# Bias attention with a cosine FFN: two V bursts per unit, one group of q/k transposes per slot

## The chip, the cores and the metric

The kernel runs on one core of a Trainium2 chip. The metric is device time in microseconds (us), the median of the runs shown; a profile comes from one further execution. TensorE is called PE in the profile, VectorE DVE, ScalarE ACT, GpSimd POOL, and SyncE, which issues the DMAs, SP. PEld is PE's loading of weights.

## The reference

All inputs are float32. Attention has 4 batches, 8 heads, 576 positions, head width 64; a small network over log-distances gives a bias for each head. Then an FFN with a cosine gate follows on 2304 tokens of width 512.

```python
scores = scale * np.matmul(q, k.transpose(0, 1, 3, 2))
x = (psi_rel / psi_i)[..., None]
bias = np.maximum(x @ w1 + b1, 0.0) @ w2
scores = scores + bias.transpose(2, 0, 1)[None, :, :, :]
attn = np.exp(scores - np.max(scores, axis=-1, keepdims=True))
attn = attn / (np.sum(attn, axis=-1, keepdims=True) + 1e-09)
out = np.matmul(attn, v)
h = x_attn @ w_in                # x_attn: out, heads side by side
result = (h * np.cos(h)) @ w_out
```

## The kernel before

Three stages follow one another. The first (to about 79 us) computes the bias table and stores it in DRAM. The second (to about 387 us) is attention, and the change lies there. The third is the FFN.

Attention works on **units**: a unit is a pair of heads (`hp`) of one batch (`b`), 16 in all, numbered 0 to 15 with the batch running fastest. A unit has five **slots**, one for each tile of queries, `tiles = [0, 1, 4, 2, 3]`: four tiles of 128 queries for each of the two heads, and tile 4, which holds the 64 left-over queries of both heads. The order of instructions is written out by hand in `slot(i)`, which software-pipelines three jobs. In slot i:

- PE computes the scores of the slot's own job (`qk`, L378, into `s`; two heads, so two tiles of two banks each, from a pool of two). DVE adds the bias and takes the minimum (L389, `neg` and `m`); the sign is turned.
- For the job of the slot before, ACT takes the exponentials (`softmax_exp`, L408), DVE adds to the sums and inverts them (`recip`, L420 and L423), and POOL multiplies (`norm`, L430).
- For the job before that, PE transposes P: eight transposes (L437, four for each head) and the left-over one (L442). The first head's four are copied to `PT` by ACT, the second head's by DVE (`keep_main`, L450 and L453), and the left-over one to `PX` by DVE.

Beside these stand four more kinds of work. The V matmuls (`pv`, L494) multiply PT and PX with V. The first half of a unit's queries has 256 columns and the second 320, and each half needs five chunks of keys: 0 to 3 from PT, 4 from PX. The two heads share the array, 64 columns each. When chunk 4 is done ACT copies the sum to `xT`. The q and k of the next unit are transposed (`turn`): `k0`, `k1`, `q0`, `q1` are four transposes for one head (`tmain`, L195, copied by ACT at L202), `kl` and `ql` are the left-over ones (`tleft`, L206, copied by ACT at L208 to L212). `swap` issues two DMAs that copy k with its halves exchanged (`kS`, L216 and L217). POOL splits q and k of coming units (`split`, L172 and L176), following `POOL_PLAN`, SP loads them (`LOAD_PLAN`), and `W_PLAN` spreads the widening of FFN weights over pairs of units: the raw load in slot 1 of even units, the absolute value on ACT in slot 0 of odd ones, DVE's steps in slots 1 and 2 of odd ones (L99, L100, L102, L104). In units 3, 7 and 11 (`b == B - 1`) every slot also loads a bias tile of the next pair of heads.

All transposes, of P as of q and k, write to one pool of three PSUM banks (`ps_t`, the name `pt` in the rows); the V sums have one bank (`ps_v`). A tile can be written when the copy out of the one three allocations earlier is done. Each engine runs its instructions in the order of the code.

The plans say what stands where. `T_EARLY` is issued between the scores and the P transposes, `T_PLAN` after the slot's copies; likewise `PV_EARLY` and `PV_PLAN`. An entry `(-1, 0, (2, 3, 4))` is: of the unit before, half 0, chunks 2 to 4. In code the V matmuls of half 0 begin at the end of slot 4 (two chunks) and end in slot 0 of the next unit (three); those of half 1 begin at the end of slot 2 and end in slot 3.

Of the kernel before, what the change touches and what calls it, by code (L numbers as in the profile page):

```python
# [28 lines left out]
def kernel(  # L29
# [42 lines left out]
    NU = len(units)  # L72
# [37 lines left out]
    with tc.manual_schedule():  # L110
# [103 lines left out]
        def kswap(u):  # L214
            t = tp.tile([128, 1216], F32R, tag="kS", name="kS")
            nc.sync.dma_start(out=f(t[0:64]), in_=f(kN[u][64:128]))  # L216
            nc.sync.dma_start(out=f(t[64:128]), in_=f(kN[u][0:64]))  # L217
            kS[u] = t

        def turn(u, ops):  # L220
            if u >= NU:
                return
            for op in ops:
                if op == "swap":
                    kswap(u)
                elif op[1] == "l":
                    tleft(u, op[0])
                else:
                    tmain(u, op[0], int(op[1]))
# [135 lines left out]
        def qk(u, j, h):  # L365
            t = tiles[j]
            s = ps_s.tile([128, 2, 512], F32, tag="s", name="s")
            if t < 4:
                o = 128 * t + 704 * h
                stats = [(qTs[u % 2][:, o : o + 128], h)]  # L370
            else:
                stats = [(qTs[u % 2][:, 512:640], 0), (qTs[u % 2][:, 576:704], 1)]
            for hf in range(2):
                n = 0
                for a, hh in stats:
                    c0 = HALF * hf + (640 if t == 4 else 576) * hh
                    for kt in (kN, kS):
                        nc.tensor.matmul(  # L378
                            s[:, hf, 0:HALF],
                            a,  # L380
                            kt[u][:, c0 : c0 + HALF],
                            start=(n == 0),
                            stop=(n == 2 * len(stats) - 1),
                        )
                        n += 1
            hp = units[u][0]
            neg = tt.tile([128, 2, HALF], F32, tag="neg", name="neg")
            m = sv.tile([128, 2], F32, tag=f"m{h}", name="m")
            nc.vector.tensor_tensor_reduce(  # L389
                neg,  # L390
                s[:, :, 0:HALF],
                bias[hp, t, h].rearrange("p (a x) -> p a x", a=2),
                1.0,
                3.0e38,
                ALU.add,
                ALU.min,
                m[:, 0:1],
            )
            cur[u, j, h] = (neg, m)
# [85 lines left out]
        def pv(u, hf, chunks):  # L485
            hp, b = units[u]
            n = vN[u % 2]
            if 0 in chunks:
                X_[u, hf] = ps_v.tile([128, 512], F32, tag="v", name="pv")
            ps = X_[u, hf]  # L490
            for c in chunks:
                for h in range(2):
                    a, m = (n[:, 4 * h + c], PT[u, hf][:, h, c, :]) if c < 4 else (n[:, 8 + h], PX[u, hf])
                    nc.tensor.matmul(  # L494
                        ps[64 * h : 64 * h + 64, 0 : WQ[hf]],
                        a,
                        m,
                        start=(c == 0),
                        stop=(c == 4),
                        tile_position=(0, 64 * h),  # L500
                        skip_group_check=True,
                    )
            if 4 in chunks:
                c0 = b * S + 256 * hf
                act_copy(xT[:, hp, c0 : c0 + WQ[hf]], X_.pop((u, hf))[:, 0 : WQ[hf]])
# [6 lines left out]
            [(2, "k", 1)],  # L512
            [(2, "k", 2)],
        ]
        T_EARLY = [["k0"], ["kl", "swap"], ["q0"], ["ql"], ["q1"]]
        T_PLAN = [["k1"], [], [], [], []]
        PV_EARLY = [[(-1, 0, (2, 3, 4))], [], [], [(-1, 1, (2, 3, 4))], []]
        PV_PLAN = [[], [], [(-1, 1, (0, 1))], [], [(0, 0, (0, 1))]]
        LOAD_PLAN = [[(2, "k")], [], [], [(2, "q")], [(1, "v")]]
        W_PLAN = [("load", 1), ("abs", 5), (0, 6), (1, 6), (2, 7), (3, 9), (4, 9)]  # L520
        get = lambda i: jobs[i] if 0 <= i < len(jobs) else None
# [2 lines left out]
        def slot(i):  # L524
            u, j = divmod(i, 5)
            now, last, prev = get(i), get(i - 1), get(i - 2)
            heads = lambda x: range(2 if tiles[x[1]] < 4 else 1)
            if now:
                qk(u, j, 0)
            if last:  # L530
                for h in heads(last):
                    softmax_exp(*last, h)
            if now and tiles[j] < 4:
                qk(u, j, 1)
            for du, hf, chunks in PV_EARLY[j]:
                if 0 <= u + du < NU:
                    pv(u + du, hf, chunks)
            turn(u + 1, T_EARLY[j])
            if i == 1:
                load_bias(0, tiles[-1])  # L540
            if prev:
                if j in (2, 4):
                    alloc_half(prev[0], j // 2 - 1)
                pt = [ptrans(*prev, h) for h in heads(prev)]
                pl = ptrans_left(*prev)
            if last:
                recip(*last, 0)
                recip(*last, 1)
            if prev:
                if len(pt) == 2:  # L550
                    keep_main(*prev, 0, pt[0])
                    keep_main(*prev, 1, pt[1])
                else:
                    keep_both(prev[0], pt[0])
            if last:
                for h in heads(last):
                    norm(*last, h)
            if prev:
                keep_left(*prev, pl)
            for du, hf, chunks in PV_PLAN[j]:  # L560
                if 0 <= u + du < NU:
                    pv(u + du, hf, chunks)
            turn(u + 1, T_PLAN[j])
            if now:
                for du, x, step in POOL_PLAN[j]:
                    if u + du < NU:
                        split(u + du, x, step)
                for du, x in LOAD_PLAN[j]:
                    if u + du < NU:
                        load(u + du, x)  # L570
                hp, b = units[u]
                if b == B - 1 and hp + 1 < HP:
                    load_bias(hp + 1, tiles[j])
                if u == NU - 1 and j < KD:
                    split_x(0, 0, j)
                for step, at in W_PLAN:
                    w, r = divmod(i - 0 - at, 10)
                    if r == 0 and 0 <= w < len(wparts):
                        if step == "load":
                            load_w(*wparts[w])  # L580
                        elif step == "abs":
                            abs_w(*wparts[w])
                        else:
                            widen_w(*wparts[w], step)
# [226 lines left out]
```

## Time and profile before

| | |
|---|---|
| runs | 800.36, 799.08, 800.66 us; median 800.36 |
| profiled execution | 803.56 us, of which the span from first to last instruction is 801.7 |
| busy, share of the span | PE 764.9 us (95%), PEld 619.2 (77%), DVE 598.4 (75%), ACT 459.1 (57%), POOL 415.4 (52%) |
| granted clock of PE | 0.995 over the span |
| attention, 79 to 387 us | PE busy 286.96 us of 308 |
| V matmuls, L494 | 512 with PT, 128 with PX |
| chain that ended last | PE 81%, ACT 7%, DMA 4%, DVE 4% |

A busy PE is a sum of intervals in which some matmul was under way; since matmuls overlap, what a group costs is read from its start to the start of the next group. The chain of waits is followed back from the last instruction, at each step to what released it. In a timeline row the first number is the start in us, the second the time from the group's first start to its last end; `x8` is the number of instructions in the row, and the bracket tells how long the engine was idle before and what ended that. An fp32 V matmul is two instructions in the trace, so a chunk of both heads is `x4`.

### The profile page before, as it was taken

Reading aid. Unit: us, or ns where it says so; the run is one execution under the profiler, and the core shown is the slowest. Engines: PE = TensorE matmul, PEld = TensorE weight load, DVE = VectorE, ACT = ScalarE, POOL = GpSimd, SP = SyncE. Lnnn points to the kernel's source line nnn. Section 1 sums busy time; section 2 is a strip of 40 time slices with the busy share of each in tenths; the row PEclk is TensorE's granted clock in tenths of the full one; section 3 lists DMA queues with packets and bytes.
Section 4 is the critical chain, followed back from the end, with each engine's and each line's share of the span. In section 5 each row is a group of like instructions: output and inputs, shape, how many; then the busy total and the mean of one; then the engine's idle time right before and its main releaser. Section 6 shows DMA issues by size and latency. Waiting matters only on the chain.

```text
span 801.7 us, 14168 instructions
## 1 busy us (share of the span) xinstructions
PE 764.9 (95%) x4882; PEld 619.2 (77%) x4882; DVE 598.4 (75%) x1300; ACT 459.1 (57%) x964; POOL 415.4 (52%) x493
## 2 busy tenths in 40 slices
PE   7899899989999999899999999999999999999997
PEld 4335677767777777677889998898888888889996
DVE  8558576757676767677577978889899898986655
ACT  5548677767777766676656555554544445443332
POOL 3324466656575657576753744637355373644400
PEclk9999999999999999999999999999999999999999
DMA  4647734673466346632001010111101011001112
GB/s 153 194 148 249 181 77 107 164 145 76 120 173 133 94 123 160 135 81 58 19 26 52 28 53 27 52 41 39 53 26 54 27 53 36 18 14 53 45 48 79
DMA packets 70599, 68.50 MB, mean 85 GB/s; under 512 B 30080, under 2 KB 54784, under 8 KB 70528
## 3 DMA queue, kind: packets, MB, share of 16 engines
q1 hardware_dynamic: 70528, 67.60, 31.1%
q8 instruction: 39, 0.64, 0.3%
q14 instruction: 32, 0.26, 0.1%
HBM read 42.00 MB, written 15.61 MB: 72 GB/s over the span
## 4 chain that ended last, share of the span: by engine, by line
PE 81%; ACT 7%; DMA 4%; DVE 4%; issue 3%; POOL 2%; SPq 0%; POOLq 0%; DVEq 0%; ACTq 0%
PE ph L613 24%; PE po L668 23%; PE pv L494 10%; PE s L378 8%; PE pa L306 7%; PE pt L437 4%; PE pt L195 3%; ACT P L408 3%; DMA bt<-sc 3%; POOL ht L301 1%; ACT kN L202 1%; PE pt L442 1%; ACT wb L91 1%; ACT PT L450 1%; DMA kS<-kN 1%
## 5 line engine op out<-in xcount | busy, mean ns | idle before, releaser
L430 POOL TENSOR_SCALAR P<-P,rc 128x576 f32<-128x576 f32 x144 | 111.1, 783 | 86.8 <-ACT PT L450 23.6
L389 DVE CUSTOM_DVE_ANT_0 neg<-s,bt 128x576 f32<-128x576 f32 x144 | 103.8, 753 | 37.4 <-PE s L378 33.3
L617 ACT ACTIVATE a<-ph,quarter 128x384 int32<-128x384 f32 x96 | 55.8, 581 | 106.6 <-PE ph L613 105.5
L408 ACT ACTIVATE P<-neg,m 128x576 f32<-128x576 f32 x144 | 110.6, 775 | 9.8 <-DVE dn L420 5.7
L480 POOL TENSOR_TENSOR xs<-xT,xs 128x384 fp32r<-128x384 f32 x96 | 107.7, 1122 | 8.0
L613 PE MATMUL ph<-xs,wpre 128*128 128x384 f32 x576 | 109.4, 338 | 0.8 <-DVE a L632 0.8
L613 PE MATMUL ph<-xs,w 128*128 128x384 f32 x576 | 108.3, 337 | 0.5 <-DVE a L632 0.5
L623 DVE SCALAR_TENSOR_TENSOR r<-a,ph 128x384 f32<-128x384 int32 x96 | 52.9, 551 | 73.1 <-ACT a L617 73.0
L613 PEld LDWEIGHTS ph<-xs,wpre 128*128 128x128 f32 x576 | 101.8, 188 | 6.2 <-DVE a L632 2.1
L613 PEld LDWEIGHTS ph<-xs,w 128*128 128x128 f32 x576 | 101.3, 188 | 5.6 <-DVE a L632 1.6
L628 ACT ACTIVATE r<-r,hpi 128x384 f32<-128x384 f32 x96 | 59.4, 619 | 69.4 <-DVE r L624 69.4
L378 PE MATMUL s<-kN,qT 128*128 128x288 f32 x320 | 94.3, 317 | 2.6 <-DVE dn L420 2.2
L378 PE MATMUL s<-kS,qT 128*128 128x288 f32 x320 | 87.1, 295 | 0.0
L437 PE MATMUL pt<-ident,P 128*128 128x128 f32 x576 | 80.7, 279 | 6.5 <-POOL P L430 6.4
L479 POOL TENSOR_SCALAR xs<-xT 128x384 fp32r<-128x384 f32 x96 | 62.0, 646 | 39.7 <-PE ph L613 39.7
L494 PE MATMUL pv<-PT,vN 128*64 128x320 f32 (+1 forms) x512 | 76.0, 419 | 0.0
L668 PE MATMUL po<-w,gh 128*128 128x512 f32 x288 | 75.3, 396 | 0.0
L668 PE MATMUL po<-wpre,gh 128*128 128x512 f32 x288 | 75.2, 396 | 0.0
L642 DVE TENSOR_TENSOR gl<-a,gh 128x384 fp32r<-128x384 f32 x96 | 74.4, 775 | 0.6 <-ACT gh L636 0.6
L306 PE MATMUL pa<-ht,nbd 128*32 128x79 f32 (+43 forms) x640 | 67.9, 419 | 6.1 <-POOL ht L301 3.6
L378 PEld LDWEIGHTS s<-kN,qT 128*128 128x128 f32 x320 | 60.9, 190 | 16.4 <-issue 9.7
L453 DVE COPY PT<-pt 128x512 f32<-128x512 f32 x64 | 43.8, 684 | 39.9 <-PE pt L437 39.8
(82 smaller groups left out, 1385.9 us busy)
## 6 DMA issues: line engine op xcount, KB each, us to landing
sc<-rt SPq DMA_DIRECT2D x36, 295.5 KB
kS<-kN SPq DMA_DIRECT2D x32, 304.0 KB
raw<-in_moe_w_in_dram SPq DMA_DIRECT2D x16, 512.0 KB
raw<-in_moe_w_out_dram SPq DMA_DIRECT2D x16, 512.0 KB
bt<-sc SPq DMA_DIRECT2D x16, 288.0 KB
nk<-in_k_dram SPq DMA_DIRECT2D x32, 128.0 KB
nq<-in_q_dram SPq DMA_DIRECT2D x32, 128.0 KB
vN<-in_v_dram SPq DMA_DIRECT2D x32, 128.0 KB
```

The lines of the kernel that those rows point to most:

```text
L306: nc.tensor.matmul(ps[32 * s : 32 * s + 32, base + a : base + b], nbd, rhs, start=True, stop=True, tile_position=(0, 32 * s),)
L378: nc.tensor.matmul(s[:, hf, 0:HALF], a, kt[u][:, c0 : c0 + HALF], start=(n == 0), stop=(n == 2 * len(stats) - 1),)
L389: nc.vector.tensor_tensor_reduce(neg, s[:, :, 0:HALF], bias[hp, t, h].rearrange("p (a x) -> p a x", a=2), 1.0, 3.0e38, ALU.add, ALU.min, m ...
L408: nc.scalar.activation(out=P[u, j][:, 576 * h : 576 * h + 576], in_=neg.rearrange("p a x -> p (a x)"), func=AF.Exp, bias=m[:, 0:1], scale= ...
L430: nc.gpsimd.tensor_scalar(p, p, r, 1.0, ALU.mult, ALU.mult)
L437: nc.tensor.transpose(ps[:, 128 * c : 128 * c + 128], p[:, o : o + 128], ident)
L479: nc.gpsimd.tensor_scalar(h, src, 1.0, 1.0, ALU.mult, ALU.mult)
L480: nc.gpsimd.tensor_tensor(l, src, f(h), ALU.subtract)
L494: nc.tensor.matmul(ps[64 * h : 64 * h + 64, 0 : WQ[hf]], a, m, start=(c == 0), stop=(c == 4), tile_position=(0, 64 * h), skip_group_check= ...
L613: nc.tensor.matmul(ps, a, x, start=(i == 0), stop=(i == 3 * KD - 1))
L642: nc.vector.tensor_tensor(gl, a, f(G[key][0]), ALU.subtract)
L668: nc.tensor.matmul(O[n][i], a[:, 128 * i : 128 * i + 128], w, start=(i0 == 0 and p == 0), stop=(i0 == GF - 1 and p == 2),)
```

## The change

The four plans become two. The V matmuls of a half stand in one place, all five chunks: half 0 in slot 0 of the next unit, half 1 in slot 3. Each slot has one place for q/k transposes, right behind the scores and ahead of the V matmuls: k0, k1, kl with the swap, q0, and ql with q1 in slots 0 to 4. So k1 moves from the end of slot 0 to slot 1, kl and the swap from slot 1 to 2, q0 from 2 to 3, and ql from 3 to 4.

```diff
-        T_EARLY = [["k0"], ["kl", "swap"], ["q0"], ["ql"], ["q1"]]
-        T_PLAN = [["k1"], [], [], [], []]
-        PV_EARLY = [[(-1, 0, (2, 3, 4))], [], [], [(-1, 1, (2, 3, 4))], []]
-        PV_PLAN = [[], [], [(-1, 1, (0, 1))], [], [(0, 0, (0, 1))]]
+        T_EARLY = [["k0"], ["k1"], ["kl", "swap"], ["q0"], ["ql", "q1"]]
+        PV_EARLY = [[(-1, 0, range(5))], [], [], [(-1, 1, range(5))], []]
...
             if now and tiles[j] < 4:
                 qk(u, j, 1)
+            turn(u + 1, T_EARLY[j])
             for du, hf, chunks in PV_EARLY[j]:
                 if 0 <= u + du < NU:
                     pv(u + du, hf, chunks)
-            turn(u + 1, T_EARLY[j])
...
-            for du, hf, chunks in PV_PLAN[j]:
-                if 0 <= u + du < NU:
-                    pv(u + du, hf, chunks)
-            turn(u + 1, T_PLAN[j])
```

PE, slot 0 of an even unit before, from the second burst of V matmuls to the scores of slot 1 (`pt` is a transpose's bank, `sk` the split k, `s` the scores; x4 of V matmuls are here two chunks of two heads):

```order
L494 MATMUL pv<-PT_3103,vN_112 64x256 x4
L494 MATMUL pv<-PX_3104,vN_112 64x256 x2
L195 MATMUL pt<-identr,sk 128x128 x4
L437 MATMUL pt<-ident,P 128x128 x8
L442 MATMUL pt<-ident,P 128x128
L195 MATMUL pt<-identr,sk 128x128 x4
L378 MATMUL s<-kN,qT_107 128x288
```

The same slot after, from the last scores of slot 0 to the first of slot 1:

```order
L378 MATMUL s<-kS,qT_107 128x288
L195 MATMUL pt<-identr,sk 128x128 x4
L494 MATMUL pv<-PT_3097,vN_112 64x256 x8
L494 MATMUL pv<-PX_3098,vN_112 64x256 x2
L437 MATMUL pt<-ident,P 128x128 x8
L442 MATMUL pt<-ident,P 128x128
L378 MATMUL s<-kN,qT_107 128x288
```

The k0 transposes went ahead of the V matmuls, the V matmuls are ten in a row in place of six, and the k1 transposes are gone from behind the left-over transpose.

ACT, slots 0 and 1 of an even unit before, from the exponentials of slot 0 to the P copy of slot 1:

```order
L408 ACTIVATE P,dn<-neg,m 128x576 x2
L450 ACTIVATE xT<-pv 128x256
L202 ACTIVATE kN<-pt 128x2x2x128
L450 ACTIVATE PT_3223<-pt 128x4x128
L202 ACTIVATE kN<-pt 128x2x2x128
L408 ACTIVATE P,dn<-neg,m 128x576 x2
L211 ACTIVATE kN<-pt 128x128
L212 ACTIVATE kN<-pt 128x64
L450 ACTIVATE PT_3223<-pt 128x4x128
```

The same after:

```order
L408 ACTIVATE P,dn<-neg,m 128x576 x2
L202 ACTIVATE kN<-pt 128x2x2x128
L450 ACTIVATE xT<-pv 128x256
L450 ACTIVATE PT_3223<-pt 128x4x128
L408 ACTIVATE P,dn<-neg,m 128x576 x2
L202 ACTIVATE kN<-pt 128x2x2x128
L450 ACTIVATE PT_3223<-pt 128x4x128
```

The copy of k1 moved from between the P copy and the exponentials of slot 1 to behind them, where kl's two copies were.

SP, slots 0 to 3 of an even unit before (`nk` and `nq` are loads of k and q, `raw` of FFN weights):

```order
L157 DMA nk<-in_k_dram 128x2x128 x2
L162 DMA nk<-in_k_dram 64x64 x2
L216 DMA kS<-kN 64x1216
L217 DMA kS<-kN 64x1216
L79 DMA raw<-in_moe_w_in_dram 128x4x256
L157 DMA nq<-in_q_dram 128x2x128 x2
```

The same after:

```order
L157 DMA nk<-in_k_dram 128x2x128 x2
L162 DMA nk<-in_k_dram 64x64 x2
L79 DMA raw<-in_moe_w_in_dram 128x4x256
L216 DMA kS<-kN 64x1216
L217 DMA kS<-kN 64x1216
L157 DMA nq<-in_q_dram 128x2x128 x2
```

The swap moved behind the load of raw weights; in units 3, 7 and 11 it moved likewise behind the three bias loads of slot 1.

## Rows read from the trace of the kernel before

**Rows 1.** Busy by stretch: stretch, length, PE PEld DVE ACT POOL, clock, DMA.
```profile
79.00:387.00 308.00, 286.96 (x2186) 219.92 (x2183) 211.20 (x639) 214.75 (x535) 192.41 (x258) 0.99 0.51 121
```

**Rows 2.** Chain of waits, 84 to 392 us: start, length, engine and line.
```profile
152.29 1.01 PE pv L494 x8
...
173.35 1.01 PE pv L494 x8
...
192.61 1.01 PE pv L494 x8
...
211.29 1.01 PE pv L494 x8
...
319.18 4.71 DMA kS<-kN
```

**Rows 3.** Timeline of PE over unit 6 (even), first rows of its groups.
```profile
194.81 1.08 PE L494 MATMUL pv<-PT,vN 128*64 128x256 f32 x8
...
196.26 0.54 PE L195 MATMUL pt<-identr,sk 128*128 128x128 f32 x4
196.63 1.06 PE L437 MATMUL pt<-ident,P 128*128 128x128 f32 x8
197.53 0.33 PE L442 MATMUL pt<-ident,P 128*128 128x128 f32 x1
...
201.04 0.33 PE L442 MATMUL pt<-ident,P 128*128 128x128 f32 x1 [0.44 <-ACT kN L212]
...
202.56 1.18 PE L437 MATMUL pt<-ident,P 128*128 128x128 f32 x8
203.57 0.32 PE L442 MATMUL pt<-ident,P 128*128 128x128 f32 x1
203.82 1.30 PE L494 MATMUL pv<-PT,vN 128*64 128x320 f32 x8
205.05 0.40 PE L378 MATMUL s<-kN,qT 128*128 128x288 f32 x1
...
206.31 1.30 PE L494 MATMUL pv<-PT,vN 128*64 128x320 f32 x8
...
208.07 0.28 PE L206 MATMUL pt<-identr,sq 128*128 128x128 f32 x1
...
209.09 0.27 PE L442 MATMUL pt<-ident,P 128*128 128x128 f32 x1
209.12 0.38 PE L378 MATMUL s<-kN,qT 128*128 128x288 f32 x1
...
210.25 0.46 PE L195 MATMUL pt<-identr,sq 128*128 128x128 f32 x4
210.55 0.63 PE L437 MATMUL pt<-ident,P 128*128 128x128 f32 x4
211.01 0.27 PE L442 MATMUL pt<-ident,P 128*128 128x128 f32 x1
```

**Rows 4.** Timeline of ACT, slots 0 to 2 of unit 6.
```profile
197.36 0.59 ACT L450 ACTIVATE PT<-pt 128x512 f32<-128x512 f32 x1
...
199.10 0.76 ACT L408 ACTIVATE P<-neg,m 128x576 f32<-128x576 f32 x1
...
200.87 0.61 ACT L450 ACTIVATE PT<-pt 128x512 f32<-128x512 f32 x1
201.35 0.80 ACT L408 ACTIVATE P<-neg,m 128x576 f32<-128x576 f32 x1
...
202.87 0.64 ACT L202 ACTIVATE qT<-pt 128x512 fp32r<-128x512 f32 x1
```

**Rows 5.** Timeline of DVE, slots 1 and 2 of unit 11 (odd).
```profile
297.19 0.53 DVE L99 TENSOR_SCALAR wb<-wb 128x512 f32<-128x512 f32 x1
...
299.26 0.75 DVE L389 CUSTOM_DVE_ANT_0 neg<-s,bt 128x576 f32<-128x576 f32 x1
```

**Rows 6.** Timeline of POOL, slots 2 and 3 of unit 4.
```profile
170.72 0.67 POOL L172 TENSOR_SCALAR sk<-nk 128x576 fp32r<-128x576 f32 x1 [5.80 <-DMA nk<-in_k_dram]
```

## The prediction

> **What bounds the kernel now.** I read the busy times by stretch first, then the chain of waits, then the timelines of PE, ACT, DVE and POOL over one unit. From 79 to 387 us, where the change lies, PE is busy for 286.96 of 308 us, DVE for 211.20, ACT for 214.75, POOL for 192.41 [rows 1]; the granted clock there is 0.99, the upper of its two levels (2.4 GHz), so nothing is to be won or lost there. The chain of waits runs over PE almost all through a unit, and its rows give the length of one, from one burst of V matmuls at the end of slot 4 to the next [rows 2]: 192.61 to 211.29 is 18.68 us (unit 6, even), 173.35 to 192.61 is 19.26 (unit 5, odd; odd units also widen weights on DVE in slot 1), 152.29 to 173.35 is 21.06 (unit 4, after a bias reload). So the sum is made on PE's order inside a unit, slot by slot, and the waits of PE are looked for one by one.
>
> **Prices of PE's pieces**, as start to start, since matmuls overlap [rows 3]. One slot's scores between transposes: 209.12 to 210.25, 1.13. Four q/k transposes: 210.25 to 210.55, 0.30; a left-over one a quarter of that, 0.07 (an estimate). Eight P transposes to the left-over one: 196.63 to 197.53, 0.90; four: 210.55 to 211.01, 0.46. Left-over to scores: 209.09 to 209.12, 0.03. Left-over to V matmuls: 203.57 to 203.82, 0.25, so entering the half-width V burst costs 0.22 more than entering scores. Of 320 columns, a burst of two chunks is 203.82 to 205.05, 1.23, and one of three is 206.31 to 208.07, 1.76: a chunk is 0.53, and each burst has 1.23 - 2 x 0.53 = 0.17 of its own. For 256 columns three chunks are 194.81 to 196.26, 1.45, and a chunk 0.8 of 0.53, 0.42.
>
> **The joined bursts.** Five chunks in one burst are 1.76 + 2 x 0.53 = 2.82 and 1.45 + 2 x 0.42 = 2.29. What the trace before does not show is a q/k transpose followed by V matmuls, and V matmuls followed by P transposes. The first I take like left-over to V matmuls, +0.15 to +0.22 on the 0.30, so 0.45 to 0.52 (I take 0.45); below nothing it can't go, as the same array change is made. The second is taken like V matmuls to q/k transposes, which is inside 1.76 and 1.45.
>
> **The slots after, without waits.** Slot 0: scores 1.13, k0 0.45, V 2.29, P 0.90, 0.03: 4.80. Slot 1: 1.13 + k1 0.30 + 0.90 + 0.03 = 2.36. Slot 2: 1.13 + kl 0.07 + 0.90 + 0.03 = 2.13. Slot 3: 1.13 + q0 0.45 + 2.82 + 0.90 + 0.03 = 5.33. Slot 4: 1.13 + ql 0.07 + q1 0.30 + 0.46 + 0.03 = 1.99. Sum 16.61 us, against 18.68 with waits before. Nothing is computed less: the 2.07 are two V bursts' own time, their effect on the scores beside them, and PE's waits, of which one is seen at 201.04 (0.44, the left-over transpose of slot 1 waits for a PSUM bank that ACT still has to empty of kl) [rows 3].
>
> **The waits that take their place.** The slots become uneven: 4.8, 2.4, 2.1, 5.3, 2.0. ACT, DVE and POOL need about as much per slot as before, so the short ones are where they show.
> (a) Slots 0 to 2, the softmax round trip: P transposes of slot 0, their copy by ACT, two exponentials, sums, normalization on POOL, P transposes of slot 2. Before, it is 196.63 to 202.56, 5.93 [rows 3]. In it ACT goes from the P copy at 197.36 to the first exponential at 199.10, 1.74, where 200.87 to 201.35, 0.48, is enough [rows 4]: the k1 transposes of slot 0 and their copy stood between. k1 leaves slot 0, so 1.26 drop out, and the round trip is 4.67. PE alone would take 0.90 + 0.03 + 2.36 + 1.13 + 0.07 = 4.49. The wait is 0.2, and 0.3 more as the second head's normalization comes behind the first's: 0.5.
> (b) The left-over transpose of slot 1 now waits for the copy of k1. ACT: P copy 0.73 after the transposes began (196.63 to 197.36), then 200.87 to 202.87, 2.00, to the copy, and 0.64 for it [rows 4]: 3.37. PE: 0.90 + 0.03 + 1.13 + 0.30 + 0.90 = 3.26. The 0.1 lies inside (a).
> (c) Slot 4 copies ql and q1 together; by the same ACT sum its left-over transpose, and the second head's scores behind it, are 0.2 late.
> An even unit: 16.61 + 0.7 = 17.3, a gain of 1.38.
> (d) In odd units the |w| pass stands behind slot 0's P copy on ACT. Priced by the nearest row, a 128x512 copy of 0.64 [rows 4], it makes (b) 0.7. DVE widens weights at the end of slot 1: 297.19 to 299.26, 2.07 [rows 5]. Behind that stands slot 2's bias-and-minimum, which frees the scores' buffer, and PE's second scores of slot 3 wait for it. Before, slots 1 and 2 took long enough to hide most of it; now they are 2.36 and 2.13, and I bound this wait between 0.4 and 1.5, taking 0.75. With (c) and 0.25 for the rest, 1.9: the unit is 18.5, a gain of 0.75.
> Seven even and eight odd units from the first on: 7 x 1.38 + 8 x 0.75 = 15.7.
>
> **What is lost again.** In units 3, 7 and 11 the next bias is loaded, and in the unit after it k's load lands late: POOL waits 5.80 us for it at 170.72 [rows 6], and unit 4 is 21.06 - 18.68 = 2.4 longer. Faster units ask for k earlier. If it landed at the same time as before, the gain of both units (2.13) would be lost three times, 6.4; if it moved with its issue, nothing. SP's queue issues the same DMAs, but PE's pace sets only part of it: I take 1.2 a time, 3.6. At the front the first unit's two V chunks (1.45 - 0.42 = 1.0) move into the second; if they lay in PE's waiting this costs up to 1.0; I take 0.5. The kS swap is issued a slot later, behind the raw weights or bias pieces that it stood ahead of on SP. It landed in 4.71 us at worst on the chain [rows 2]; slots 3 and 4 give 7.3 before the first scores that read it, so it costs nothing, and q's load, queued behind SP's wait for kl, has a unit's time. V's load, in slot 4, needs the V buffer of the unit before, read last in slot 3 as it was. Without that cover, a unit would lose what kS lands beyond 7.3.
>
> Sum: 15.7 - 3.6 - 0.5 = 11.6 less. The profiled run is 803.56, so 792.0; against the median, 800.36, it is **788.8 us**, the forecast. Its own range: 782 where (d) waits 0.4 and no reload loses anything, 797 where the V entry is 0.52 and (d) waits 1.5.
>
> **A rule that speaks against it.** PE's wait at 201.04 is the same in most units: 0.44 for a bank [rows 3]. The Trainium skill (Perfetto Trace Analysis, Identifying the Most-Contended Engine) says that one gap that repeats on the engine that should be saturated can mean too few buffers in PSUM or SBUF. By it the gap would stay, since three banks and 20 transposed tiles a unit stay. That is the slower rival.
>
> **The rivals.**
> Slower, the bank wait in every slot: before, slots held 5, 4, 4, 4 and 3 transposed tiles; now each holds four on three banks, so the left-over one always takes the bank of the slot's own q/k transposes, which ACT empties only after two exponentials. If PE waits the 0.44 of [rows 3] five times, an even unit is 16.61 + 2.2 = 18.8 and an odd one 19.4: 15 x 0.13 slower, and 4.1 from reloads and start: 806. It decides from 0.4 a slot. Against it: slots 0 and 3 have 2.3 and 2.8 us of V matmuls between the copy's turn and that transpose. Chance 0.10.
> All waits vanish: units of 16.6 gain 7 x 2.07 + 8 x 2.65 = 35.7, less 6.4 and 0.5: 771.5. For it: two-slot sums differ by tenths. Against it: DVE's 2.07 in a slot of 2.36. Chance 0.12.
> DMA takes it: k lands no earlier (6.4 lost), and kS, behind bias or raw weights, comes a short slot (2.36) late after each reload, 7.1: 15.7 - 6.4 - 7.1 - 0.5 = 1.7 gained, 798.7. Chance 0.10.
> No change, the waits in between: (a) to (d) at 1.4 in even and 2.5 in odd units, 16.61 + 1.4 = 18.0 and 19.1, gain 5.9 less 4.1 to 6.9: 800. Chance 0.08.
> That the change doesn't do what it says is ruled out by PE's order: the bursts stand there as one.
>
> **How the numbers follow.** Forecast 0.60, and the rivals as above. 0.2% (1.6 us) is about what a measurement of this kernel can tell from no change. Faster: 0.60 + 0.12 + half of the DMA case, 0.77; same: 0.08 + 0.05, 0.13; slower 0.10. The range takes in the forecast's own, the DMA and no-change cases, and the near part of the fast one: 777 to 801.
>
> **What would show it.** V in two rows a unit of about 2.3 and 2.8 us; units of 17.3 and 18.5 by the chain; no wait for kl's second copy of 0.44 in slot 1, small ones for k1's copy and for POOL's P in slot 2; in odd units, DVE's widening just ahead of PE's scores of slot 3. Wrong would be: left-over transposes that wait in slots 1, 2 and 4 for ACT by 0.4 or more (the bank rival), scores that wait for kS, or V bursts well over 2.8.

## The result and the profile after

The changed kernel took 811.43 us (median of four runs, 804.02 to 815.54) beside 800.51 for the kernel before in the same comparison: a ratio of 1.0119, interval 1.0073 to 1.0165. It is slower, by some 9 to 11 us, where 788.8 with a range to 801 had been forecast. The profiled run of after took 810.62 us, its span is 808.8 us against 801.7 of before: 7.1 us, which the two traces can be asked for.

The stretch of [rows 1], in the kernel after (columns as there):

```profile
79.00:387.00 308.00, 277.79 (x2135) 220.69 (x2130) 207.90 (x621) 210.23 (x522) 185.69 (x251) 0.96 0.51 120
```

PE is busy 9 us less in the same 308 us, has done less in them (2135 matmuls against 2186), and the granted clock has gone from 0.99 to 0.96. The next line is the first of what the matmuls and weight loads of the scores (L378) waited for in after (us, times).

```profile
  DMA kS<-kN: 37.0, 12
```

Matmul and weight load wait side by side here, so the 37.0 is not a path length. The matmuls by themselves stood 19.3 us for kS: 8.03 in unit 1, 3.32, 2.64 and 2.07 in units 5, 9 and 13, and 0.40, 0.64 and 2.16 in units 4, 8 and 12. Before, kS isn't among what these scores wait for. To see what that costs, the span is cut at the first scores of each unit. Three such units of after: 1, 5 and 6.

```profile
90.69:119.05 28.36, 19.51 (x142) 15.36 (x141) 14.51 (x43) 13.88 (x35) 12.07 (x17) 0.82 0.53 104
174.05:197.45 23.40, 19.25 (x142) 15.03 (x141) 13.93 (x41) 13.52 (x35) 12.15 (x17) 0.93 0.46 94
197.45:215.40 17.95, 17.40 (x140) 13.95 (x141) 13.12 (x39) 13.68 (x35) 12.52 (x17) 1.00 0.45 115
```

And units 1, 5 and 6 of before, cut the same way:

```profile
92.39:115.29 22.90, 19.74 (x139) 14.93 (x140) 15.44 (x47) 14.24 (x35) 11.96 (x16) 0.93 0.47 105
174.29:193.56 19.27, 18.14 (x142) 13.87 (x140) 13.94 (x42) 13.54 (x35) 11.19 (x16) 1.00 0.36 83
193.56:212.23 18.67, 18.09 (x141) 13.85 (x140) 12.62 (x38) 13.43 (x35) 12.57 (x18) 1.00 0.42 110
```

Unit 6 has gained 0.72 us. Units 1 and 5, which have the two longest waits for kS, have lost 5.46 and 4.13. Over all sixteen: the seven ordinary units (2, 3, 6, 7, 10, 11, 14) gained 5.9, unit 0 1.9, and units 4, 8 and 12, with the reloaded bias, 2.6; units 1, 5, 9 and 13, one behind the first load or a reload, lost 5.46 + 4.13 + 3.57 + 2.84 = 16.0; and from unit 15's first scores to the FFN's first matmul it takes 20.69 in place of 19.64. That is 16.0 + 1.05 - 10.4 = 6.7 of the 7.1.

How a unit like the fifth begins shows in the chain of waits of after (start, length, engine and line):

```profile
168.08 9.63 DMA kS<-kN
177.71 0.04 issue
177.75 1.71 PE s L378 x7
179.46 0.47 PE pt L195 x4
179.93 3.15 PE pv L494 x20
```

The swap takes 9.63 us from its issue to where PE goes on. [Rows 2] had one such row, 4.71. And the V burst behind it takes 3.15, where the same 20 matmuls take 2.31 in unit 6: PE is slow after the wait. In unit 1 the wait is longest. The stretches around it, 94 to 99, 99 to 104 and 104 to 109 us:

```profile
94.00:99.00 5.00, 0.00 (x0) 0.00 (x0) 0.76 (x6) 0.87 (x2) 2.15 (x3) 0.50 0.89 151
99.00:104.00 5.00, 4.91 (x27) 3.88 (x29) 1.78 (x6) 0.63 (x1) 1.51 (x3) 0.59 0.29 78
104.00:109.00 5.00, 4.52 (x41) 3.83 (x36) 3.14 (x10) 4.09 (x10) 2.52 (x4) 1.00 0.00 0
```

PE does nothing for five microseconds, and the clock stands at 0.50, the lower level. Over the next five it is 0.59, so it is at that level for most of them: PE is busy 4.91 us and gets 27 matmuls done. After that it is back at 1.00.

Why kS is late: SP's queue behind a reload, in unit 4, first before and then after (start, time at the queue, line, transfer).

```profile
162.65 0.52 SPq L216 DMA_DIRECT2D kS<-kN  x1
163.24 0.57 SPq L217 DMA_DIRECT2D kS<-kN  x1
163.85 0.90 SPq L79 DMA_DIRECT2D raw<-in_moe_w_in_dram  x1
```

```profile
166.79 0.58 SPq L79 DMA_DIRECT2D raw<-in_moe_w_in_dram  x1
167.54 0.49 SPq L216 DMA_DIRECT2D kS<-kN  x1
168.08 0.59 SPq L217 DMA_DIRECT2D kS<-kN  x1
```

Counted from the unit's first scores (153.23 and 155.15), the swap left 9.4 us into the unit before and 12.4 us into it after, now behind 512 KB of weights. That is more than the one slot. In unit 6 of after, with no reload ahead of it, the swap leaves as soon as kl's copies are done (206.89 and 206.91), 9.5 us into the unit; in unit 4 SP issues it 2.3 us after them (165.25 and 167.54). A swap is 128 packets of 4,864 bytes, by which it can be followed: from the issue of its second half to the last packet it takes 8.58 us before and 8.65 after, as long in both. (The packets of units 8 and 12 give 7.57 and 7.83 before, 8.29 and 7.77 after.) PE goes on about 1 us after the last packet, at 176.73 and 177.75. So kS is there about 18.6 us into the unit before, which is 21.06 us long, and 21.6 us into it after, where PE is through at 18.9. In before, PE also stood 2.18 us near the end of unit 4 for POOL's P, which was late behind k's load [rows 6], and kS landed in that time (171.82). In after that wait is 0.38, and PE meets kS instead. In unit 0 the swap itself became slow: 3.6 us before, 10.5 after, behind the early bias pieces and the first weights.

Inside an ordinary unit the change did what was forecast of it. PE in unit 6, first rows of some groups, beside [rows 3]:

```profile
198.59 0.46 PE L195 MATMUL pt<-identr,sk 128*128 128x128 f32 x4
198.98 1.95 PE L494 MATMUL pv<-PT,vN 128*64 128x256 f32 x16
...
201.29 1.09 PE L437 MATMUL pt<-ident,P 128*128 128x128 f32 x8
...
203.68 1.06 PE L437 MATMUL pt<-ident,P 128*128 128x128 f32 x8
204.69 0.33 PE L442 MATMUL pt<-ident,P 128*128 128x128 f32 x1
...
205.91 0.22 PE L206 MATMUL pt<-identr,sk 128*128 128x128 f32 x1
206.63 1.38 PE L437 MATMUL pt<-ident,P 128*128 128x128 f32 x8 [0.49 <-POOL P L430]
207.84 0.27 PE L442 MATMUL pt<-ident,P 128*128 128x128 f32 x1
...
209.39 2.37 PE L494 MATMUL pv<-PT,vN 128*64 128x320 f32 x16
...
212.24 1.09 PE L437 MATMUL pt<-ident,P 128*128 128x128 f32 x8
```

The joined bursts are 201.29 - 198.98 = 2.31 and 212.24 - 209.39 = 2.85 (2.29 and 2.82 in the sum), and k0 ahead of the first 0.39 (0.45). The left-over transpose of slot 1 no longer waits 0.44 for kl's copy: it starts 1.01 after the eight P transposes began, which take 0.90 to 0.93. That holds for even units. In odd ones this wait was longer, and half of it is left, now for k1's copy. Slot 1 of unit 7, before and then after:

```profile
220.27 0.33 PE L442 MATMUL pt<-ident,P 128*128 128x128 f32 x1 [0.99 <-ACT kN L212]
```

```profile
223.17 0.33 PE L442 MATMUL pt<-ident,P 128*128 128x128 f32 x1 [0.48 <-ACT kN L202]
```

New in unit 6 is a wait of 0.49 in slot 2, for POOL. POOL's timeline tells why:

```profile
204.28 1.57 POOL L176 TENSOR_TENSOR sq<-nq,sq 128x320 fp32r<-128x320 f32 x2
205.82 1.47 POOL L430 TENSOR_SCALAR P<-P,rc 128x576 f32<-128x576 f32 x2
```

The q split of slot 0 stands ahead of slot 1's normalization, which starts at 205.82, when the split is done, and the P transposes of slot 2 wait for it.

### The profile page after: what moved, and what is told of

Read it like the earlier page. It is cut to its first block, busy times and chain, and to the rows that moved or that the text cites. A ratio compares the mean times of both kernels' runs of the same rounds, so it can differ in the third digit from the quotient of the medians.

```text
span 808.8 us, 14154 instructions
## 1 busy us (share of the span) xinstructions
PE 762.7 (94%) x4882; PEld 625.0 (77%) x4882; DVE 600.4 (74%) x1300; ACT 460.0 (57%) x964; POOL 414.3 (51%) x493
## 4 chain that ended last, share of the span: by engine, by line
PE 71%; DMA 10%; DVE 6%; ACT 5%; POOL 4%; issue 2%; SPq 0%; POOLq 0%; DVEq 0%; ACTq 0%
PE ph L607 24%; PE po L662 23%; DMA kS<-kN 8%; PE pv L494 8%; PE pa L306 6%; PE s L378 4%; PE pt L437 3%; ACT P L408 2%; POOL P L430 2%; DVE neg L389 1%; PE pt L195 1%; POOL ht L301 1%; DVE wb L100 1%; ACT wb L91 1%; DVE PT L453 1%
## 5 line engine op out<-in xcount | busy, mean ns | idle before, releaser
L378 PE MATMUL s<-kS,qT 128*128 128x288 f32 x320 | 89.9, 302 | 19.3 <-DMA kS<-kN 19.3
L378 PE MATMUL s<-kN,qT 128*128 128x288 f32 x320 | 96.6, 322 | 3.1 <-DVE m L389 3.1
L437 PEld LDWEIGHTS pt<-ident,P 128*128 128x128 f32 x576 | 61.6, 141 | 23.3 <-POOL P L430 11.0
L378 PEld LDWEIGHTS s<-kS,qT 128*128 128x128 f32 x320 | 61.7, 193 | 20.7 <-DMA kS<-kN 17.7
L494 PE MATMUL pv<-PT,vN 128*64 128x320 f32 (+1 forms) x512 | 74.3, 436 | 0.3 <-ACT PT L450 0.3
```

What stands on the lines that cost most here:

```text
L378: nc.tensor.matmul(s[:, hf, 0:HALF], a, kt[u][:, c0 : c0 + HALF], start=(n == 0), stop=(n == 2 * len(stats) - 1),)
L437: nc.tensor.transpose(ps[:, 128 * c : 128 * c + 128], p[:, o : o + 128], ident)
L494: nc.tensor.matmul(ps[64 * h : 64 * h + 64, 0 : WQ[hf]], a, m, start=(c == 0), stop=(c == 4), tile_position=(0, 64 * h), skip_group_check= ...
```

## The experiments

Theory 1: the loss is the later swap, and the joined bursts by themselves gain what ordinary units show. Rivals: the uneven slots are at fault (2), or the DMA engines are full whoever issues what and when (3). The kernel before ran beside each group of runs, and each ratio is to it, with its 95% interval; its medians there were 802.16 (e1 to e4), 803.87 (e5 to e8), 804.38 (e9 to e12), 802.70 (e13 to e15) and 803.79 (e16). Lengths of units are those of the one profiled execution of each kernel.

**The two halves of the change apart.** `e1_v_alone` joins the V bursts and leaves the transposes where they were:

```diff
-        T_EARLY = [["k0"], ["k1"], ["kl", "swap"], ["q0"], ["ql", "q1"]]
+        T_EARLY = [["k0"], ["kl", "swap"], ["q0"], ["ql"], ["q1"]]
+        T_PLAN = [["k1"], [], [], [], []]
```

> The two joined V bursts alone; the q/k transposes and the swap stand in the slots of the kernel before. Theory 1 (the loss is the swap that leaves a slot later, so that kS lands after the next unit's first scores in units 1, 5, 9 and 13; the joined bursts themselves gain what the ordinary units of the changed kernel gained, 0.7 to 1.0 us each): 15 units x 0.85 = 12.8 off 800.5, so 787 to 790, and no wait for kS over 1 us at the head of units 1, 5, 9, 13. Theory 2 (the uneven slots that the joined bursts make are at fault): 800 or more, with the long units still there.

`e2_t_alone` is the reverse: the transposes of after, V in four bursts.

```diff
-        PV_EARLY = [[(-1, 0, range(5))], [], [], [(-1, 1, range(5))], []]
+        PV_EARLY = [[(-1, 0, (2, 3, 4))], [], [], [(-1, 1, (2, 3, 4))], []]
+        PV_PLAN = [[], [], [(-1, 1, (0, 1))], [], [(0, 0, (0, 1))]]
```

> The moved transposes and swap alone; V in four bursts as in the kernel before. Theory 1: the waits for kS in units 1, 5, 9 and 13 stay (5.5 + 4.1 + 3.6 + 2.8 = 16 us) and the gain of the bursts is missing: 808 to 817. Theory 2: within 3 us of 800.5, kS in time.

Measured: 802.65 us (1.0004, 0.9987 to 1.0021) and 802.96 us (1.0017, 0.9985 to 1.0048). Neither half alone costs anything, and neither brings anything. Theory 1 falls in its plain form. Theory 2 had both times (800 or more, and within 3 us) but not what it gave for them: the ordinary units of e1 are shorter, and kS is late in e2. The units tell more than the times. In e1 no unit waits for kS for more than 0.6 us; units 6 and 7 are 17.96 and 19.11, and unit 8, with the reloaded bias, is 21.40:

```profile
230.35:251.75 21.40, 18.08 (x142) 14.51 (x141) 12.52 (x42) 14.01 (x35) 12.76 (x18) 0.97 0.79 164
```

The chain of that unit begins with a transfer, q's load, for which POOL's split waits:

```profile
229.11 7.75 DMA nq<-in_q_dram
...
237.03 0.68 POOL sq L172
```

So joined bursts alone save 0.7 in even units and 0.14 in odd ones, and the time is given back in units 1, 5, 8 and 9 and at the end. In e2 the swap is late too, units 1 and 5 are 27.97 and 20.30, but unit 5 loses only 1.03 to the kernel before, and PE keeps its clock of 1.00 there:

```profile
176.46:196.76 20.30, 18.17 (x142) 13.97 (x140) 13.89 (x42) 13.77 (x35) 11.46 (x16) 1.00 0.43 94
```

Its ordinary units gain 0.35 and 0.86, which pays for that. So it takes both: one slot less of lead for kS, and units that are shorter.

**Order on the queue, or full DMA engines.** `e3_swap_act` issues the swap from ACT:

```diff
-            nc.sync.dma_start(out=f(t[0:64]), in_=f(kN[u][64:128]))
-            nc.sync.dma_start(out=f(t[64:128]), in_=f(kN[u][0:64]))
+            nc.scalar.dma_start(out=f(t[0:64]), in_=f(kN[u][64:128]))
+            nc.scalar.dma_start(out=f(t[64:128]), in_=f(kN[u][0:64]))
```

> The changed kernel, with the two swap transfers issued by ScalarE instead of SyncE, in the same slot. Theory 1 in its form 'order of the queue' (the swap waits behind the bias and weight loads that SyncE issued before it): kS lands 3 to 4 us after its issue in every unit, the four waits vanish, 788 to 793. Theory 3 (the DMA engines themselves are full of the loads, whoever issues): kS still takes 7 to 10 us in units 0, 4, 8, 12, time 806 to 812.

`e4_loads_behind` moves the weight load and unit 0's early bias load behind the swap:

```diff
-        W_PLAN = [("load", 1), ("abs", 5), (0, 6), (1, 6), (2, 7), (3, 9), (4, 9)]
+        W_PLAN = [("load", 2), ("abs", 5), (0, 6), (1, 6), (2, 7), (3, 9), (4, 9)]
-            if i == 1:
+            if i == 2:
                 load_bias(0, tiles[-1])
```

> The changed kernel, with the weight load a slot later (behind the swap of slot 2) and the one early bias load of unit 0 also behind it. If what was issued in slot 1 holds the swap up: unit 1 loses 2 us or less in place of 5.5, and units 5, 9 and 13 come back as well, 789 to 794. If it is the bias reload issued through units 3, 7 and 11: unit 1 comes back and the other three keep their 10 us, 800 to 806.

e3 came to 812.03 (1.0119, 1.0096 to 1.0142), and that is not the plain verdict for theory 3 that it looks like. Units 5 and 9 did come back (18.69 and 18.67): in units 4 and 8 the swap issued by ACT lands in 5.0 and 3.9 us, where it took 8.7 and 8.3 in after. What was lost instead is in units 3, 7 and 11. ACT's timeline in unit 7:

```profile
224.45 0.47 ACTq L216 DMA_DIRECT2D kS<-kN  x1
232.72 0.47 ACTq L217 DMA_DIRECT2D kS<-kN  x1
233.24 0.60 ACT L450 ACTIVATE PT<-pt 128x512 f32<-128x512 f32 x1 [8.82 <-DMA kS<-kN]
```

ACT held its second issue for 8.3 us; the chain puts a bias transfer of 9.81 us ahead of it. Everything that ACT had to do stood behind, and that unit took 24.14 us. This keeps e3 from telling how much of the lateness is the queue's. Unit 3 took 5.6 us longer than in after, so the weights left SP 6.9 us into unit 4 and not 11.6, and the swap left later behind them. Counted from the weights' issue, kS has landed after 8.6 us in units 4 and 8, where the changed kernel has 9.9: some 1.3 us are what another queue can have given, and the rest of what units 5 and 9 won goes with the time that units 3 and 7 lost. The Trainium skill (DMA: Bandwidth & Descriptors, Queues, rings and completion order) says that SP and ACT each have one ring on each of the same 16 DMA engines, and that an engine takes turns between rings. The 1.3 us fit that, but no run here shows it by itself.

e4 came to 801.51 (0.9976, 0.9945 to 1.0007), 10 us below after. Unit 1 is 23.46 and units 5 and 9 are 18.29 and 18.27. But that is not for a faster swap behind the reload, which still takes 7.8 us in unit 8 and 7.3 in unit 12 (4.2 in unit 4): units 4, 8 and 12 take 21.2 to 21.8, since transfers are late one unit earlier, and that leaves kS its time. Unit 13 is still 20.40. A pair such as 4 and 5 is 39.6 us, against 42.3 in after and 40.3 before.

**Without the reload.** That leads to theory 4: PE's gain is real, and the transfers around a reload eat it, by way of kS, q, k or the bias. `e7_after_noreload` and `e8_before_noreload` take the reload away from either kernel, so that every pair of heads gets the bias of the first:

```diff
                 if b == B - 1 and hp + 1 < HP:
-                    load_bias(hp + 1, tiles[j])
+                    for h in heads((u, j)):
+                        bias[hp + 1, tiles[j], h] = bias[hp, tiles[j], h]
```

> The changed kernel without the bias reload: the tiles of the first pair of heads serve all four pairs, so 26.5 of the 35 MB of bias loads and their share of the DMA engines are left out. Theory 4: kS lands 3 to 4 us after its issue in units 4, 8 and 12, units 5, 9 and 13 come to 18.3, units 4, 8, 12 to 18.0; unit 1 stays long (its loads are kept): 811.4 - 13.5 - 4.7 = about 793. Theory 1 in its bare form (a swap that leaves a slot later is late wherever it stands): units 5, 9, 13 stay over 20, time over 803.

> The kernel before, likewise without the bias reload. Theory 4: units 4 and 12 lose their 2.4 us over the ordinary 18.7, the rest stays: 802.2 - 4.7 = 797 to 798, so that the changed kernel without a reload is 3 to 5 us faster than this one although it is 9 us slower with it. If the joined bursts and not the transfers were at fault, the changed kernel would stay slower here too.

Measured: 793.80 (0.9865, 0.9827 to 0.9903) and 797.47 (0.9910, 0.9882 to 0.9938). Without the reload the changed kernel is 3.7 us faster than the one before without it, as theory 4 said. (What is left out was overstated there: three reloads of nine tiles of 288 KB are 7.8 MB of bias, not 26.5.) The swap lands in 3.6 us in unit 4, with the weights still ahead of it, so it is the reload that made it 8.6. Every unit from 2 on now repeats. Units 5 and 6 of after without a reload, then of before without it:

```profile
173.38:191.68 18.30, 17.46 (x141) 14.00 (x141) 14.33 (x43) 13.69 (x35) 11.94 (x16) 1.00 0.35 84
191.68:209.64 17.96, 17.39 (x140) 13.94 (x141) 13.13 (x39) 13.67 (x35) 12.54 (x17) 1.00 0.44 115
```

```profile
171.32:190.55 19.23, 18.09 (x141) 13.84 (x139) 13.94 (x42) 13.58 (x35) 11.93 (x17) 1.00 0.34 80
190.55:209.23 18.68, 18.11 (x141) 13.85 (x139) 12.65 (x39) 13.43 (x35) 12.55 (x18) 1.00 0.42 111
```

The change is worth 0.93 in an odd and 0.72 in an even unit: from unit 2 to unit 15 246.3 us came down to 235.4, 10.9. Unit 1 kept its 28.55, since its own loads were kept; that and the end are why only 3.7 of the 10.9 show.

**The weight loads.** `e5_raw_moved` (on after) and `e6_v_alone_raw_moved` (on e1) move the eight weight loads, with their widening, out of the units with a fresh bias:

```diff
+        W_AT = [6, 11, 26, 31, 46, 51, 66, 71]
                 for step, at in W_PLAN:
-                    w, r = divmod(i - 0 - at, 10)
-                    if r == 0 and 0 <= w < len(wparts):
+                    w = W_AT.index(i - at + 1) if i - at + 1 in W_AT else -1
+                    if w >= 0:
```

> The changed kernel, its eight weight loads (512 KB each) moved out of the units in which the bias tiles are reloaded: slots 6, 11, 26, 31, 46, 51, 66, 71 in place of 1, 11, 21 to 71. Theory 4 (PE's gain is real, but the transfers around a reload - bias, q/k loads, weights, swap - fill the DMA engines, and kS lands late behind them): the waits for kS in units 1, 5, 9, 13 fall from 8, 4.1, 3.6 and 2.8 us lost to under 1, and units 4, 8, 12 to some 18.5 to 20; 811.4 - 13 - 3 = about 793 to 798. Theory 5 (the bias reload and the q/k loads fill them without the weights): units 4, 8, 12 stay near 21 and kS late, 805 to 811.

> The joined V bursts alone (swap in slot 1 as in the kernel before), with the weight loads moved as in the run beside this one. Theory 4: units 4, 8, 12 fall from 20.2, 21.4, 19.7 to about 18.5, unit 1 from 24.0 to about 22, unit 9 from 20.0 to 18.9: 802.65 - 4.8 - 2 - 1 = 793 to 796. Theory 5: 800 to 803.

e5 came to 801.80 (0.9977, 0.9944 to 1.0010; single runs between 796.36 and 807.57), e6 to 801.54 (0.9980, 0.9950 to 1.0009). For e5 that is 10 us off after, so theory 5, by which nothing would change, falls, but 4 to 9 us short of what theory 4 gave. In the profiled run of e5 unit 5, undisturbed and without a widening, is 17.37, while unit 4 is still 21.30: PE waits 1.11 us for kS at its start and 2.08 for POOL's P near its end. In unit 1 it waits 4.93 for kS. e6's miss is of another kind: units 2 and 3 both widen weights now, 19.1 each, and units 4, 8 and 12 stay at 19.8 to 20.5.

**What the clock costs.** `e9_fill` gives PE transposes that nobody reads ahead of the first scores of units 1, 5, 9 and 13:

```diff
+        FILL = {1: 60, 5: 24, 9: 20, 13: 16}
+            if now and j == 0 and u in FILL:
+                pf = bank(F32R)
+                for _ in range(FILL[u]):
+                    nc.tensor.transpose(pf[:, 0:128], identr, identr)
             if now:
                 qk(u, j, 0)
```

> The changed kernel with idle-time work for TensorE: 60, 24, 20 and 16 transposes of the identity ahead of the first scores of units 1, 5, 9 and 13, whose result nobody reads, about as long as the wait for kS there. If part of the loss is the clock that falls after the idle time (units 5, 9, 13 have 19.2 to 19.4 us of busy PE where undisturbed ones have 17.4): the granted clock stays 1.00 there, the three units come down by 1.5 to 2 us each and unit 1 by 2 or more, 811.4 - 7 = 803 to 806. If the clock costs nothing beyond the wait: no change, 810 to 813.

Measured: 808.72 (1.0072, 1.0036 to 1.0109), 2.7 below after where 6 to 8 were expected, and the two intervals overlap. Units 4 (with the filling work at its end) and 5:

```profile
155.21:177.24 22.03, 19.96 (x165) 16.21 (x165) 13.21 (x44) 16.23 (x40) 14.15 (x20) 1.00 0.75 171
177.24:196.63 19.39, 17.73 (x142) 14.05 (x141) 13.06 (x37) 11.45 (x30) 10.39 (x14) 1.00 0.40 91
```

The clock stays at 1.00 in these two units (units 1 and 8 are at 0.93), and PE's busy time in unit 5 goes from 19.25 to 17.73. Units 4 and 5 together are 41.42 against 42.30, so 0.88 of the 1.52 shows. Of the other pairs one fell by 2.13 (12 and 13), and two rose, by 0.61 (0 and 1) and 1.07 (8 and 9). PE still waited for kS, 0.84 us in unit 5: the filling work took the place of part of the wait. So, as far as this run goes, the wait is the larger part of the loss, and the clock a smaller one, whose size (2.7, with these intervals) is not settled.

**Is it the slot?** Theory 6 puts the runs so far together: it takes both, the later slot and the shorter units. `e13_swap_slot1` is the whole change, with the swap back in slot 1:

```diff
-        T_EARLY = [["k0"], ["k1"], ["kl", "swap"], ["q0"], ["ql", "q1"]]
+        T_EARLY = [["k0"], ["k1", "kl", "swap"], [], ["q0"], ["ql", "q1"]]
```

> The whole change but one thing: the second k group and the left-over group and the swap stand together in slot 1, so that the swap leaves in the slot in which it left before. Theory 6 (it takes both, the later slot and the shorter units: kS gets one short slot less of lead while the transfers around a reload stretch it to 8 to 10 us): kS lands in time in units 5, 9 and 13, which come to 18.3, unit 1 to 24 or less; what stays are units 4, 8, 12 at 20 to 21: 797 to 802. Theory 7 (the transfers are late whatever the slot): units 1, 5, 9, 13 still long, 808 to 812.

Measured: 801.13 (0.9968, 0.9943 to 0.9992), 10 us below after and 0.3% below before, as theory 6 said. No wait for kS over 0.3 us is left in the trace. Units 6 and 7 are 17.98 and 18.70, and units 4, 8 and 12, at 21.47, 20.49 and 19.94, are about what theory 6 left: near their ends PE waits 2.21, 2.53 and 1.39 us for POOL's P, as it did before in units 4 and 12 (2.18 and 2.47). Units 5, 9 and 13, for which theory 6 gave 18.3, are 19.88, 20.50 and 19.17, the first two at a clock of 0.95 and 0.92 behind those waits; that was missed. The slot by itself is not the cause, since e4 and e5 keep the swap in slot 2 and come to the same time: the later slot costs what it does together with what stands ahead of the swap.

**Versions meant to be faster.** Five spread the widening over slots on top of the moved weight loads (the last of them now in slot 69); all but e15 also put two of the three steps of the q split into slot 1. e10 and e15 stand on e1, e11 on after, e12 on before, e14 on e13.

```diff
-        W_PLAN = [("load", 1), ("abs", 5), (0, 6), (1, 6), (2, 7), (3, 9), (4, 9)]
+        W_PLAN = [("load", 1), ("abs", 5), (0, 6), (1, 7), (2, 8), (3, 9), (4, 11)]
-            [(1, "q", 0), (1, "q", 1), (1, "q", 2)],
-            [],
+            [(1, "q", 0)],
+            [(1, "q", 1), (1, "q", 2)],
```

> A version meant to be faster: joined V bursts, q/k transposes and swap as in the kernel before, weight loads out of the reload units, the widening steps a slot apart (VectorE's in slots 1, 2, 3 after the load in place of 1, 1, 2; GpSimd's subtraction in slot 6), and the second and third steps of the q split in slot 1. The eight units with a widening fall from 19.1 to about 18.2 us: 801.5 - 7 = 792 to 796. If VectorE and GpSimd only wait elsewhere for it: 799 to 803.

> The same loads, widening and split, on the whole change (swap in slot 2). Theory 4: ordinary units about 18.0, units 4, 8, 12 between 19 and 21 with kS late in some executions: 792 to 799. If the later swap still decides: 800 or more, and slower than the run with the swap in slot 1 beside it.

> The same loads, widening and split on the kernel before (V in four bursts): what of the gain belongs to them. Theory 4: the joined bursts are worth 0.7 us in each of 15 units less 1.05 at the end where the transfers no longer stand in the way, so this run lies 6 to 10 us above the joined one with the swap in slot 1: 800 to 803. If the joined bursts are worth nothing: equal to that run within 2 us.

> A version meant to be faster: as the run beside it, with the weight loads out of the reload units, their widening a slot apart and two steps of the q split in slot 1 (q is transposed in slot 3 here, so it isn't waited for). Theory 6: ordinary units 17.4 to 18.4, units 4, 8, 12 about 20, no wait for kS: 790 to 797. Theory 7: 800 or more.

> The joined V bursts alone (transposes and swap as in the kernel before), weight loads moved and their widening a slot apart, the q split left in slot 0: in the earlier form of this with the q split moved, TensorE waited for the split in slot 2 in every unit (26 and 23 us in all). Theory 6: that wait is gone, the eight units with a widening fall from 19.1 to about 18.3: 794 to 798. If the widening only moves the wait: 800 to 803.

They came to 821.73, 801.38, 826.94, 806.04 and 804.82 (ratios 1.0235, 0.9974, 1.0319, 1.0027 and 1.0017); all missed what was expected, e11 by the least. (e12 was there to be compared with e10.) e10 and e12 carry a mistake of mine: with the transposes of the kernel before, q0 stands in slot 2, and waits for the split that I had moved to slot 1. In e10:

```profile
PE pt L195 <- POOL sq L176: 22.8, 15, 2.5
```

Their difference, 5.2 us in favour of the joined bursts, is near the 6 to 10 that was expected, but both stand under that wait. In e14 and e15 units with a widening take 19.0 to 19.7: spread, it costs PE there as much as in one slot, or more. In e11 it is the other way: these units take 17.84 and 18.47, against 18.28 and 18.77 in e5, and what takes that back is units 4, 8 and 12, at 23.16, 21.10 and 23.48 (21.30, 20.29 and 19.74 in e5).

The last version, `e16_swap_slot1_raw`, takes only what had helped: the swap in slot 1 (as e13) and the weight loads out of the reload units (as e5).

> A version meant to be faster: the whole change with the swap in slot 1 (as in e13_swap_slot1) and the weight loads out of the reload units (as in e5_raw_moved), nothing else moved. Theory 6: no wait for kS, units 4, 8, 12 at 19.5 to 20.5 and units 5, 9, 13 at 17.4 to 18 for want of a widening, the start as in e13: 794 to 799. If the transfers of the reload units stay the bound without the weights: 800 to 803.

Measured: 796.57 (0.9907, 0.9870 to 0.9944; runs between 791.71 and 800.24). This one beats both kernels, by 0.9% and about 2%. Units 4 and 9 of it:

```profile
152.42:172.36 19.94, 17.48 (x141) 14.07 (x141) 13.42 (x42) 14.00 (x35) 12.26 (x17) 1.00 0.72 160
248.72:266.10 17.38, 17.01 (x142) 13.99 (x141) 11.01 (x35) 12.87 (x33) 11.55 (x17) 1.00 0.49 122
```

A unit with nothing in its way (9) is at 17.38, and kS isn't waited for. Unit 4, with DMA engines busy for 0.72 of it, is still 2.6 above that; 1.98 of it is a wait for POOL's P. Unit 5, given at 17.4 to 18, is 18.87, at a clock of 0.91 behind that wait.

## Why the prediction was wrong

**The step that failed** is the one on the swap: "It landed in 4.71 us at worst on the chain [rows 2]; slots 3 and 4 give 7.3 before the first scores that read it, so it costs nothing". The 4.71 was not a landing time. The row, with the one behind it in the chain:

```profile
319.18 4.71 DMA kS<-kN
323.90 0.08 DVE PX L453
```

It ends where DVE copies PX, which reads nothing of that swap, and the swap's own packets run on to 327.02, 7.83 us after the issue. In units 4 and 8 of before they take 8.58 and 7.57, where most others have 3.6 to 3.7. With these numbers, all in the trace of before, 7.3 would have been too little behind each reload. The 7.3 was mis-sized too: in after it is 8.0 in unit 6, but 6.0 in unit 4, where SP is late. So 6.0 stand against 8.65 and the 1 us to PE's next matmul. e13, which puts the swap back into slot 1, is at 0.9968 of before, where after is at 1.0119.

**The DMA rival** named this mechanism ("a short slot (2.36) late after each reload"), but sized it at 2.36 a time for three reloads, and so came out at 798.7. Measured are 4.13, 3.57 and 2.84 of loss, and 5.46 at a fourth place that it didn't name: behind the very first load of the bias, where early bias pieces and weights stand ahead of the swap too.

**"Nothing is to be won or lost there"**, said of the clock, held only as long as PE was never idle for long. In the changed kernel units 1, 5, 9, 12 and 13 run at 0.82 to 0.93; before, unit 1 alone did, at 0.93. By e9 it is the smaller part.

**The reloads.** 1.2 a time, 3.6 in all, were taken off for k landing late. The reload costs the kernel before 0.9% (e8) and the changed one 2.5% (from 1.0119 to 0.9865 of before). It isn't k alone: e1 meets q's load first, and after meets kS. In after POOL waits for k's load once, 3.3 us, where before had 5.80 and 6.08.

**The ordinary units** were right in mechanism, off in size: 0.72 against 1.38 in even ones, 0.93 against 0.75 in odd ones, 10.9 over 13 units where the same terms give 7 x 1.38 + 6 x 0.75 = 14.2. The bursts were right to hundredths (2.31 and 2.85 for 2.29 and 2.82), and so, from scores to scores in unit 6, were slots 0 and 3 (4.80 and 5.32 for 4.80 and 5.33) and slot 4 with (c) (2.21 for 2.19). In even units the waits were mis-sized: 17.96 - 16.61 = 1.35 in place of 0.7, and most of it is (a). Slot 2 takes 3.10, 0.97 over its 2.13 where (a) had 0.5: the P transposes begin 0.72 after kl's (0.07 in the sum) and take 1.21 (0.90), both for POOL's P, with the q split ahead of the normalization. The sum had priced the softmax round trip by ACT and by PE, and not POOL's queue. In odd units DVE's widening just ahead of the scores of slot 3 was there as forecast, with less to wait (0.37 in unit 7, for 0.75).

**The end.** Not in the sum at all: 1.05 us from unit 15's first scores to the FFN. It belongs to the joined bursts: that stretch takes 19.6 us in before, e2 and e8, which have four bursts, and 20.7 to 20.9 in the ten kernels that have joined ones and the widening where it was in a unit (after, e1, e3 to e7, e9, e13, e16). In before a V burst of 1.22 stands just ahead of the scores of slot 3; joined, it comes behind them, and PE waits 0.55 there for DVE. The other half is open.

**The bank rival**, chance 0.10 for slower, was not what happened. In slot 1 of unit 6 the left-over transpose waits 0.1, and not 0.44. The prediction read this wait as "the same in most units", but that was so for even units alone: in odd ones before had 0.99 to 1.02, and after has 0.45 to 0.48 (0.7 in (d)). In the other slots of an ordinary unit it waits for ACT 0.2 at most. The rule that went with it (the Trainium skill, Perfetto Trace Analysis; it stands there under Optimization Strategy: the same gap repeating can mean that there is too little SBUF or PSUM for the next tile) would have kept the gap. Here a new order at the same number of banks left a quarter of it in even units and half in odd ones.

## What to carry to other kernels

Before a transfer is moved later, take its landing time from its own packets, in the unit where the DMA engines are fullest, and set it against the lead that is left in the shortened unit; a row in the chain of waits need not end where the transfer lands. When compute between two bursts of transfers gets shorter, the transfers' own time doesn't, so a gain per unit must be summed over units with full DMA engines apart. And two edits that each measure as nothing can lose together, when one takes the lead of a transfer and the other the time that covered for it.

## What was not expected of the hardware

In 5 us without a matmul the granted clock stood at 0.50, and the next 5 us ran at 0.59, with 27 matmuls where the 5 us after that had 41; the idle 3.3 us of unit 5 left a V burst at 3.15 that takes 2.31 at a clock of 1.00. The second of a swap's two transfers of 304 KB lands 3.4 to 3.7 us after its issue in nine of the units 1 to 14 of e7 (up to 5.3 in the others), and took 7.6 to 10.5 in before and after behind a reload or the first loads. And an engine that issues a transfer can be held by what the issue waits for: ACT stood 8.3 us at its second one, with all its work behind it.
